# A two-layer attention and GEGLU kernel: first row tile in fp32 from raw weights, seven more transposed on TensorE, all loads in one queue, and a new order

## The chip, the core and the metric

The kernel runs on one core of a Trainium2 chip. A core has five engines with instruction streams of their own: TensorE (PE, matrix products; its weight loads are listed as PEld), VectorE (DVE), ScalarE (ACT), GpSimd (POOL) and SyncE (SP, which here only issues transfers). TensorE reads SBUF and writes PSUM; 16 DMA engines move data between HBM and SBUF. SyncE and ScalarE each have a DMA queue. The metric is the time of one execution on the device in microseconds; lower is better.

## What is computed

Two layers over x of 2048 rows and 512 columns in fp32, with the same weights in both: x is normalised, goes through attention and is added back; it is normalised again, goes through a gated feed forward and is added back.

```python
def _A_ref(x, wqkv, wo):          # D = 512, H = 32 heads of 16
    W, dil = 8, 2
    qkv = (x @ wqkv)              # split into q, k, v
    idx = pos[:, None] - off[None, :]      # off = 0, 2, ..., 14
    logits = jnp.einsum("bhsd,bhswd->bhsw", q, kg) * scale
    logits = jnp.where(mask, logits, -1e9)
    attn = _softmax(logits, axis=-1)
    o = jnp.einsum("bhsw,bhswd->bhsd", attn, vg)
    return o_as_rows @ wo
def _B_ref(x, w_gate, w_up, w_down):       # F = 1792
    return (_gelu(x @ w_gate) * (x @ w_up)) @ w_down
x = A_x
x = x + _A_ref(_layernorm(x), A_wqkv, A_wo)
x = x + _B_ref(_layernorm(x), B_w_gate, B_w_up, B_w_down)
# and both once more
```

Each position looks at itself and at seven positions before it, two apart. So even and odd rows never meet in attention, and the kernel treats them as two sequences of 1024.

## The kernel before

**Tiles.** Each layer is cut into eight chunks of two row tiles of 128 rows (`CHUNKS`, even and odd rows in turn, J = 2). A chunk goes through three functions:

- `attention_inputs(l, c, prio)`: loads the chunk's rows tile by tile into `xa` (three buffers), takes their mean and variance (`norm`: VectorE for the statistics, then a short chain for the inverse root, on VectorE for the very first chunk and on GpSimd for the others, one chain for both tiles), and calls `normed` for each tile. That writes the normalised tile `xn` on ScalarE, and `split_transpose` makes of it two f16 halves, `hl`: the rounded value (ScalarE) and the remainder (GpSimd, L777). A DMA transpose (SyncE, L781) turns both into `ax`, with the contraction on the partitions. The projection to q, k, v is done for each half of the heads, h, and each tile, j: 12 matmuls of 512 and 12 of 256 columns (L801): high times high, high times low and low times high, over four blocks of the contraction. ScalarE moves the result out of PSUM (L840, `stg`), and SyncE stores it to `qkvd` in HBM (L851).
- `attention(l, c, T)`: for each of four groups of eight heads loads windows of q, k and v from `qkvd` (L878) with their halo of earlier rows, and does logits, softmax and the weighted sum on VectorE (with the exponential on ScalarE). The result is split and turned by a DMA transpose into `ot`.
- `feed_forward(l, c, T, ot, mark)`: the output projection with `w_o`, the residual, a norm, a DMA transpose into `bx`, then seven steps of gate and up products into PSUM `pg`, gelu and product, a split into `gh`, and the down products into `pd`; the sum goes to `xs` (layer 0) or `out` (layer 1).

**Weights.** All matmuls work in f16 with split operands. Each weight is loaded raw in fp32, its largest magnitude is found (`absmax` on VectorE or `abssum` on ScalarE), a power of two is made of it (`exponents`: reductions, transposes on PE at L398, small VectorE operations), and `split` writes the scaled high half (ScalarE, L443) and the low half (VectorE, L448) in f16. wqkv comes in two halves of four blocks each (`prep_q(0)` and `prep_q(1)`), and its raw blocks lie in the buffer of `w_d`. The loads of wqkv are issued by SyncE; those of the gate, up, output and down weights by ScalarE (`on="ACT"` in `load`, L482): 16 of 448 KB, 4 and 14 of 256 KB.

**The halo of the first rows.** The rows ahead of the sequence in `qkvd` are filled with zeros by eight DMAs that ScalarE issues (L636).

**The order.** Nothing is emitted at once. Every step is a node in a graph with an engine, an estimated occupancy, what it reads and writes, the buffers it takes, and a priority. `plan` places the nodes one after another: each time the one that could start earliest by its model; among those that could start within a short time of that, the one of lowest priority. The instructions are then emitted in that order, and every engine works through its own in order. The priorities come from the table `AT`; `ahead` (8.5 tiles) says for how many tiles of layer 0 the inputs of attention have a place of their own ahead of the feed forward. `start` and `step` set the nominal times T of the chunks. `plan` models the DMA engines as a rate of 370 bytes per ns, shared by two queues, with a limit on how much is queued ahead in each.

Of the kernel before, what the change touches and what calls it, by code (L numbers as in the profile page):

```python
# [17 lines left out]
P = 128  # L18
# [72 lines left out]
DMA_FIXED = 1.8  # L91
QUEUE = {"SP": 3.0, "ACT": 1.0}
DEPTH = 3.6
WAIT, SOON = 0.3, 20.0
DMA_RATE = 0.37e3


class Graph:
# [4 lines left out]
    def add(self, where, occ, fn, r=(), w=(), prio=0.0, get=(), order=(), done=None, kb=None, table=None, urgent=False, after=0.0):  # L103
# [3 lines left out]
        n.land, n.size, n.urgent, n.after = done, kb, urgent, after  # L107
# [40 lines left out]
    def plan(self):  # L148
# [15 lines left out]
        dma, port_free, table = {"SP": 0.0, "ACT": 0.0}, 0.0, None  # L164
        placed, todo = [], len(self.nodes)
        while todo:
            best = None
            for e, ns in cand.items():
                at = []
                for n in ns:  # L170
                    t = max(free[e], n.ready, port_free if n.port else 0.0)
                    if n.size is not None and not n.urgent:
                        t = max(t, dma[e] - QUEUE[e])
# [31 lines left out]
            if n.size is not None:  # L205

                other = "ACT" if e == "SP" else "SP"
                free[e] = max(free[e], dma[e] - DEPTH)
                begin = max(t + occ, dma[e])
                both = min(max(0.0, dma[other] - begin), 2 * n.size / DMA_RATE)  # L210
                dma[e] = begin + n.size / DMA_RATE + both / 2
                dma[other] += both / 2
                n.done = dma[e] + DMA_FIXED
            else:
                n.done = t + (occ if n.land is None else occ - n.occ + n.land) + LAG[e]
# [40 lines left out]
def t_mm(n):  # L256
    return 0.0025 + n / 2400


T_SMALL = 0.17  # L260
T_ISSUE = 0.45
T_XPOSE = 1.3
LATE = 1e6
# [3 lines left out]
def dilated_attention_geglu(ctx: ExitStack, tc: tile.TileContext, x, wqkv, wo, wg, wu, wd, out):  # L267
# [99 lines left out]
    P_st = pool("stg", 3, [P, 3, HH, P])  # L367
# [11 lines left out]
    P_pr = Pool("prod", [prod], fifo=False)  # L379
    pd_flat = P_pd.tiles[0].rearrange("p j c -> p (j c)")  # L380
# [98 lines left out]
    def load(dst, src, kb, w, prio, r=(), on="SP"):  # L479
        eng = nc.sync if on == "SP" else nc.scalar  # L480
        return g.add(
            on, T_ISSUE, lambda: eng.dma_start(dst, src), r=r, w=w, kb=kb, prio=prio,  # L482
            after=AT["bulk"] if on == "ACT" else 0.0,
        )
# [20 lines left out]
    def prep_q(h, prio, early):  # L505
# [18 lines left out]

        g.add("DVE", 3 * T_SMALL, rest, r=[(f"q{h}", "e")], w=[("s_log", h)], prio=prio + 50)
# [4 lines left out]
    def load_f(h, prio):  # L530
        for k in range(KT):
            for key, w, src in (("g", w_g, wg), ("u", w_u, wu)):
                src = src.rearrange("(k p) (h c) -> h k p c", p=P, h=2)
                i = h * KT + k
                load(w.raw(i), src[h, k], 448, [(f"r{key}", i)], prio + 0.1 * k, on="ACT")

    def prep_f(h, prio, how):
# [17 lines left out]
        for k in range(KT):  # L555
            for n, (key, w) in enumerate((("g", w_g), ("u", w_u))):
                i = h * KT + k
                pre = [(key, i - 1)] if i else []
# [21 lines left out]
    def prep_o(prio, how, early):  # L580
        for k in range(KT):
            load(w_o.raw(k), wo[k * P : (k + 1) * P], 256, [(P_o_lease, k)], early, on="ACT")
# [13 lines left out]
    def load_d(prio):  # L596
        for i in range(NF):
# [3 lines left out]
                r=[("q", b) for b in range(2 * KT)], on="ACT",  # L601
# [22 lines left out]
    zeros = P_k.tiles[0].rearrange("p r c -> p (r c)")[0:16, 0 : HALO * P]  # L624
    z_lease = Lease(P_k)
    for l in range(2):
        dst = qkvd[l].rearrange("a h t r c -> (a h) t r c")[:, 2:6, 0:HALO]
        if l == 0:
            g.add(
                "POOL", 1.6, lambda: nc.gpsimd.memset(zeros, 0.0), w=[(z_lease, 0)],  # L630
                get=[z_lease], prio=-2000,
            )
        for a in range(4):
            g.add(
                "ACT", 0.35,
                lambda dst=dst, a=a: nc.scalar.dma_start(  # L636
# [535 lines left out]
```

## Time and profile before

| | |
|---|---|
| runs | 1274.81, 1277.32, 1278.92 us, median 1277.32 |
| span of the profiled execution | 1280.5 us |
| PE busy | 1226.0 us, 96% |
| VectorE busy | 994.7 us, 78% |
| ScalarE busy | 488.4 us, 38% |
| GpSimd busy | 402.0 us, 31% |
| mean granted TensorE clock | 0.988 |
| moved by DMA | 176.09 MB |

A row of a timeline has the start in us, the duration, the engine, the line of the kernel, the operation, what it writes and reads, shapes, a count where several are merged, and in brackets how long the engine was idle before and what ended that. The names are the program's own: `ax<-hl` is the DMA transpose of an attention input, `qkvd<-stg` a store of projections, `xa` a loaded row tile; raw wqkv blocks appear as `w_d`, in whose buffer they lie. A group row ends with busy us and the mean ns of one, and the idle time before. The chain of waits has the start, the duration, and what the end of the kernel was waiting for in that time. Matmuls are pipelined and their ends are modelled: in a dense stretch the distance of starts, not the duration, is what one costs.

### The profile page before, as it was taken

Reading aid. Unit: us, or ns where it says so; the run is one execution under the profiler, and the core shown is the slowest. Engines: PE = TensorE matmul, PEld = TensorE weight load, DVE = VectorE, ACT = ScalarE, POOL = GpSimd, SP = SyncE. Lnnn points to the kernel's source line nnn. Section 1 sums busy time; section 2 is a strip of 40 time slices with the busy share of each in tenths; the row PEclk is TensorE's granted clock in tenths of the full one; section 3 lists DMA queues with packets and bytes.
Section 4 is the critical chain, followed back from the end, with each engine's and each line's share of the span. In section 5 each row is a group of like instructions: output and inputs, shape, how many; then the busy total and the mean of one; then the engine's idle time right before and its main releaser. Section 6 shows DMA issues by size and latency. Waiting matters only on the chain.

```text
span 1280.5 us, 21381 instructions
## 1 busy us (share of the span) xinstructions
PE 1226.0 (96%) x8650; PEld 848.9 (66%) x8650; DVE 994.7 (78%) x1435; ACT 488.4 (38%) x746; POOL 402.0 (31%) x388
## 2 busy tenths in 40 slices
PE   3689799999999999999999999999999999999998
PEld 1345367586767676765776676767766676676775
DVE  5568889998898989998988958888888788685111
ACT  4366265343434444333433243333334242332211
POOL 2233227443243423431433142322313222042211
PEclk9899899999999999999999999999999999999999
DMA  9999952554545372529534393334354262621000
GB/s 236 266 280 329 227 158 81 142 160 117 172 101 164 97 211 82 152 84 247 140 99 126 110 241 93 105 101 130 105 151 120 85 186 44 202 62 42 17 17 17
DMA packets 201794, 176.09 MB, mean 138 GB/s; under 512 B 108224, under 2 KB 168640, under 8 KB 201696
## 3 DMA queue, kind: packets, MB, share of 16 engines
q1 hardware_dynamic: 196736, 162.57, 45.7%
q10 hardware_dynamic: 4960, 12.18, 3.5%
q8 instruction: 67, 1.10, 0.4%
q14 instruction: 31, 0.25, 0.1%
HBM read 115.87 MB, written 33.67 MB: 117 GB/s over the span
## 4 chain that ended last, share of the span: by engine, by line
PE 90%; DMA 8%; DVE 1%; SPq 1%; ACT 0%; issue 0%; POOL 0%; DVEq 0%; ACTq 0%
PE pg L801 67%; PE pd L1089 23%; DMA ax<-hl 3%; DMA qkvd<-stg 2%; DMA xa<-in_A_x_dram 1%; DMA v<-qkvd 1%; DMA w_d<-in_A_wqkv_dram 0%; DMA bx<-hl 0%; ACT stg L840 0%; DVE x L1102 0%; SPq L878 0%; SPq L482 0%; SPq L781 0%; DVE x L1008 0%; DVE nw L697 0%
## 5 line engine op out<-in xcount | busy, mean ns | idle before, releaser
L801 PE MATMUL pg<-bx,w_g 128*128 128x256 f16 x2688 | 330.0, 273 | 0.4 <-DMA bx<-hl 0.4
L801 PE MATMUL pg<-bx,w_u 128*128 128x256 f16 x2688 | 330.1, 273 | 0.0
L1089 PE MATMUL pd<-w_d,gh 128*128 128x512 f16 x1344 | 306.7, 379 | 0.0
L801 PEld LDWEIGHTS <-w_g 128*128 128x128 f16 x2688 | 262.8, 98 | 49.1 <-issue 0.6
L801 PE MATMUL pg<-w_q,ax 128*128 128x512 f16 (+1 forms) x1536 | 267.6, 336 | 28.1 <-DMA ax<-hl 23.4
L1078 POOL TENSOR_TENSOR gh<-g,gh 128x512 f16<-128x512 f32 x112 | 166.1, 1483 | 409.2 <-ACT gh L1073 406.2
L801 PEld LDWEIGHTS <-w_u 128*128 128x128 f16 x2688 | 262.8, 98 | 30.6
L801 PEld LDWEIGHTS <-ax 128*128 128x128 f16 x1536 | 153.0, 100 | 142.7 <-DMA ax<-hl 27.9
L1089 PEld LDWEIGHTS <-gh 128*128 128x128 f16 x1344 | 131.4, 98 | 139.9
L1064 DVE SCALAR_TENSOR_TENSOR g<-pg,small,g 128x512 f32<-128x512 f32 (+1 forms) x128 | 85.8, 681 | 141.1 <-ACT g L1056 138.9
L1056 ACT ACTIVATE g<-pg,small 128x512 f32<-128x512 f32 (+1 forms) x128 | 79.4, 633 | 270.7 <-PE pg L801 260.3
L955 DVE TENSOR_TENSOR prod<-v,lg 128x1024 f32<-128x1024 f32 x128 | 168.7, 1349 | 1.2
L777 POOL TENSOR_TENSOR hl<-xn,hl 128x512 f16<-128x512 f32 x64 | 86.5, 1358 | 237.8 <-ACT hl L773 213.6
L896 DVE TENSOR_TENSOR prod<-k,q 128x2048 f32<-128x2048 f32 x64 | 148.6, 2322 | 7.0 <-DMA k<-qkvd 6.3
L966 DVE TENSOR_TENSOR prod<-prod 128x1024 f32<-128x1024 f32 (+1 forms) x128 | 150.6, 1176 | 1.6
L903 DVE TENSOR_REDUCE lg<-prod 128x128 f32<-128x2048 f32 x64 | 145.9, 2279 | 0.9
L777 POOL TENSOR_TENSOR hl<-o,hl 128x256 f16<-128x256 f32 x64 | 79.0, 1235 | 176.3 <-ACT hl L773 166.7
L840 ACT ACTIVATE stg<-pg 128x768 f32<-128x768 f32 x64 | 51.2, 807 | 128.1 <-PE pg L801 125.1
L1073 ACT CAST gh<-g 128x512 f16<-128x512 f32 x112 | 68.9, 616 | 78.8 <-DVE g L1064 75.5
L801 PE MATMUL pg<-w_o,ot 128*128 128x512 f16 x384 | 85.5, 379 | 0.0
L1056 ACT ACT_TABLE_LOAD x41 | 52.6, 1283 | 34.4 <-PE pg L801 34.0
L801 PEld LDWEIGHTS <-ot 128*128 128x128 f16 x384 | 37.6, 98 | 42.1
(78 smaller groups left out, 678.8 us busy)
## 6 DMA issues: line engine op xcount, KB each, us to landing
k<-qkvd SPq DMA_DIRECT2D x64, 576.0 KB, 5.3
v<-qkvd SPq DMA_DIRECT2D x64, 576.0 KB, 3.5
qkvd<-stg SPq DMA_DIRECT2D x64, 384.0 KB, 4.8
q<-qkvd SPq DMA_DIRECT2D x64, 128.0 KB, 2.3
xa<-in_A_x_dram SPq DMA_DIRECT2D x16, 256.0 KB, 4.5
x<-in_A_x_dram SPq DMA_DIRECT2D x8, 512.0 KB
xs<-x SPq DMA_DIRECT2D x8, 512.0 KB, 3.5
xa<-xs SPq DMA_DIRECT2D x16, 256.0 KB, 5.9
```

The lines of the kernel that those rows point to most:

```text
L777: "POOL", t_pool(n), lambda: nc.gpsimd.tensor_sub(lo(), src(), hi()),
L801: nc.tensor.matmul(pt, a, b, start=i == 0, stop=i == n - 1)
L840: lambda pg=pg, stg=stg: nc.scalar.activation(stg.tile().rearrange("p t g c -> p (t g c)"), pg.tile().rearrange("p b c -> p (b c)")[:, 0:768],
L896: nc.vector.tensor_mul(pr, win, q.tile()[:, 0:J].unsqueeze(2).to_broadcast([P, J, W, P]))
L903: lambda lgv=lgv: nc.vector.tensor_reduce(lgv(), pr.rearrange("p j w (h d) -> p j w h d", d=DH), axis=AX.X, op=ALU.add),
L955: lambda j=j, v=v, lg=lg: nc.vector.tensor_mul(prod[:, j].rearrange("p w (h d) -> p w h d", d=DH), v.tile()[:, j : j + W].rearrange("p w ( ...
L966: lambda a=a, b=b: nc.vector.tensor_add(pr[:, :, 0:a], pr[:, :, 0:a], pr[:, :, a:b]),
L1056: lambda sel=sel, h=h, pg=pg, gt=gt: nc.scalar.activation(gt.tile()[:, sel, 0:N], pg.tile()[:, sel, 0:N], AF.Gelu_apprx_tanh, scale=cst["s ...
L1064: lambda sel=sel, h=h, pg=pg, gt=gt: nc.vector.scalar_tensor_tensor(gt.tile()[:, sel, 0:N], pg.tile()[:, sel, JM * P : JM * P + N], cst["c ...
L1073: lambda gt=gt, gh=gh: nc.scalar.copy(gh.tile()[:, 0, :, 0:N], gt.tile()[:, :, 0:N]),
L1078: lambda gt=gt, gh=gh: nc.gpsimd.tensor_sub(gh.tile()[:, 1, :, 0:N], gt.tile()[:, :, 0:N], gh.tile()[:, 0, :, 0:N]),
L1089: nc.tensor.matmul(pd.tile()[:, j], gh.tile()[:, a, i, cs], wd_of(f, b), start=f == 0 and n == 0, stop=f == NF - 1 and n == 2,)
```

## The change

- **First row tile.** `NRAW` = 1: tile 0 of layer 0 is projected with fp32 matmuls from the raw weights. A new `turned` makes `xn` as before and transposes its four blocks on PE into a PSUM buffer of `pg`; `turned_whole` moves the result to `xf` in SBUF, a piece of `w_g`'s buffer that isn't written until the two projections are done (`("x0", h)`). The projection has 8 matmuls for each half of the heads in place of 24, and the scale that the split would have applied to the weights is applied when ScalarE empties PSUM (`s_raw`).
- **Tiles 1 to 7** of layer 0 (`NPE` = 8): the transposes are done on PE as well; ScalarE writes the f16 high part from PSUM, and VectorE the remainder. The GpSimd subtraction and the DMA transpose of these tiles go.
- **The first chunk** has a norm for each of its two tiles, on VectorE for the first and on GpSimd for the second.
- **Loads**: all are issued by SyncE. The zero fill is one DMA per layer.
- **The model of `plan`** has one DMA queue; each transfer has a time for its shape (x 1.55 us for two tiles, a store of projections 1.25, k and v 1.65, q 0.4, a transpose of four blocks 0.96, weights by 330 bytes per ns). `AT` has new numbers throughout; `ahead` is 17.1 tiles. `stg` buffers are no longer taken strictly in turn.

```diff
-    lq0=-1.2, lq1=-1.3, lf0=5.0, lo=42.0, lf1=44.3, ld=60.0, pq0=-787.8, pq1=9.2, pf0=26.2, po=53.4, pf1=62.0,
-    pd=130.5, x0=-1000.0, first=-1.4, tile=12.1, ahead=8.5, lead=190.5, norm=300.0, proj=10.1, half=18.4,
-    row=12.4, att=90.0, hg1=6.5, hg2=12.0, kv=13.7, xl=28.1, gu=5.4, bulk=8.0, start=51.1, step=39.1,
+    lq0=-167.4, lq1=-34.0, lf0=-158.4, lo=122.2, lf1=232.9, ld=421.6, pq0=-172.6, pq1=-218.4, pf0=-37.8,
+    po=-41.1, pf1=67.7, pd=70.0, x0=-1490.1, first=-77.3, tile=6.1, ahead=17.1, lead=339.3, norm=23.4,
+    proj=-32.1, half=129.8, row=-113.0, att=76.2, hg1=9.7, hg2=7.9, kv=-12.0, xl=406.6, gu=5.9, bulk=167.5,
+    start=28.2, step=41.3,
...
-    def load(dst, src, kb, w, prio, r=(), on="SP"):
-        eng = nc.sync if on == "SP" else nc.scalar
+    def load(dst, src, kb, w, prio, r=()):
         return g.add(
-            on, T_ISSUE, lambda: eng.dma_start(dst, src), r=r, w=w, kb=kb, prio=prio,
-            after=AT["bulk"] if on == "ACT" else 0.0,
+            "SP", T_ISSUE, lambda: nc.sync.dma_start(dst, src), r=r, w=w, us=kb / RATE, prio=prio,
         )
...
+    def turned(x_of, norm_l, scale_bias, j, prio, get=()):
+        xn = scaled(x_of, norm_l, scale_bias, j, prio)
+        lease = Lease(P_pg)
+        view = lambda: lease.tile()[:, 0].rearrange("p (k c) -> p k c", k=KT)
+        def turn():
+            for k in range(KT):
+                nc.tensor.transpose(view()[:, k], xn.tile()[:, k * P : (k + 1) * P], ident)
+        g.add("PE", T_TURN, turn, r=[(xn, 0)], w=[(lease, 0)], get=[lease, *get], prio=prio)
+        return lease, view
...
+    def turned_split(x_of, norm_l, scale_bias, j, dst, w, get, prio):
+        pt, view = turned(x_of, norm_l, scale_bias, j, prio, get)
+        g.add(
+            "ACT", t_act(D), lambda: nc.scalar.copy(dst()[:, 0], view()),
+            r=[(pt, 0)], w=w, prio=prio,
+        )
+        g.add(
+            "DVE", t_dvp(D), lambda: nc.vector.tensor_sub(dst()[:, 1], view(), dst()[:, 0]),
+            r=[(pt, 0)], w=w, prio=prio,
+        )
...
+                def project_whole(h=h, pg=pg, xf=xf):
+                    pt = pg.tile().rearrange("p b c -> p (b c)")
+                    for kt in range(KT):
+                        for lo, hi in span:
+                            nc.tensor.matmul(
+                                pt[:, lo:hi], xf.tile()[:, kt * P : (kt + 1) * P],
+                                w_q.raw(h * KT + kt)[:, lo:hi], start=kt == 0, stop=kt == KT - 1,
+                            )
...
+        cst["s_raw", h], mk_raw = power(e, -1, 268 + LQ)
...
+        if l + c == 0:
+            norms = [norm([xt[j]], prio - AT["norm"] + j, "POOL" if j else "DVE") for j in range(J)]
+            norms = [(nl, lambda j, f=f: f(0)) for nl, f in norms]
+        else:
+            norms = [norm(xt, prio - AT["norm"], "POOL")] * J
```

More of the change, by code (lines that the diff above doesn't have):

```diff
@@ L101, in __init__, with add @@
         self.writer, self.readers = {}, {}
-    def add(self, where, occ, fn, r=(), w=(), prio=0.0, get=(), order=(), done=None, kb=None, table=None, urgent=False, after=0.0):
+    def add(self, where, occ, fn, r=(), w=(), prio=0.0, get=(), order=(), done=None, us=None, table=None, urgent=False, after=0.0):
         n = Node()
@@ L163, in plan @@
         free = dict.fromkeys(LAG, 0.0)
-        dma, port_free, table = {"SP": 0.0, "ACT": 0.0}, 0.0, None
+        dma, port_free, table = 0.0, 0.0, None
         placed, todo = [], len(self.nodes)
@@ L205, in plan @@
             if n.size is not None:
[L207 to L213, printed above, removed]
+                free[e] = max(free[e], dma - DEPTH)
+                dma = max(t + DMA_ISSUE, dma) + n.size
+                n.done = max(dma + DMA_FIXED, t + occ + DMA_FIXED)
             else:
@@ L262 @@
 T_XPOSE = 1.3
+T_TURN = 0.8
+NRAW, NPE = 1, 8
 LATE = 1e6
@@ L534, in load_f @@
                 i = h * KT + k
-                load(w.raw(i), src[h, k], 448, [(f"r{key}", i)], prio + 0.1 * k, on="ACT")
+                load(w.raw(i), src[h, k], 448, [(f"r{key}", i)], prio + 0.1 * k)
     def prep_f(h, prio, how):
@@ L581, in prep_o @@
         for k in range(KT):
-            load(w_o.raw(k), wo[k * P : (k + 1) * P], 256, [(P_o_lease, k)], early, on="ACT")
+            load(w_o.raw(k), wo[k * P : (k + 1) * P], 256, [(P_o_lease, k)], early)
         for k in range(KT):
@@ L600, in load_d @@
                 w_d.raw(i), wd[i * P : (i + 1) * P], 256, [("rd", i)], prio + 0.1 * i,
-                r=[("q", b) for b in range(2 * KT)], on="ACT",
+                r=[*(("q", b) for b in range(2 * KT)), ("x0", 0), ("x0", 1)],
             )
@@ L819, in attention_inputs @@
                 pg, stg = Lease(P_pg), Lease(P_st)
+                whole = n0 + j < NRAW
+                span = ((0, 512), (512, 768))
                 def project(h=h, j=j, pg=pg):
```

123 lines of the change are left out of this document (78 added, 45 removed).

## The prediction

> **What bounds the kernel now.** I read the windows of the trace first, cut where TensorE (PE) stops being full, then PE's timeline, then the chain of waits. Columns of the windows: stretch, us, busy time of PE, its weight loads (PEld), VectorE, ScalarE and GpSimd with their instructions, granted clock of PE, mean share of the 16 DMA engines, GB/s.
>
> ```profile
> 0.00:42.00 42.00, 12.20 (x51) 5.85 (x52) 23.49 (x59) 18.68 (x27) 11.28 (x30) 0.97 1.06 224
> 42.00:162.00 120.00, 101.20 (x561) 56.61 (x560) 91.26 (x161) 59.84 (x107) 34.31 (x50) 0.91 1.02 282
> 162.00:1275.00 1113.00, 1112.63 (x8040) 786.43 (x8040) 878.50 (x1215) 409.85 (x613) 356.39 (x308) 1.00 0.42 119
> ```
>
> From 162 to 1275 us PE has 1112.6 of 1113 us of work: nothing but less PE work can shorten that part. Before 162 the DMA engines are full and PE is not. How much PE time is lost there has to be counted in PE's pace, since busy time holds the modelled ends of matmuls. The groups by form give the counts, the end of the chain the pace:
>
> ```profile
> L801 PE MATMUL pg<-bx,w_u 128*128 128x256 f16 x2688 | 330.1, 273 | 0.0
> L801 PE MATMUL pg<-bx,w_g 128*128 128x256 f16 x2688 | 330.0, 273 | 0.4 <-DMA bx<-hl 0.4
> L1089 PE MATMUL pd<-w_d,gh 128*128 128x512 f16 x1344 | 306.7, 379 | 0.0
> L801 PE MATMUL pg<-w_q,ax 128*128 128x512 f16 x768 | 188.1, 398 | 28.1 <-DMA ax<-hl 23.4 <-ACT stg L840 2.5 <-DVE lg L930 2.3
> L801 PE MATMUL pg<-w_q,ax 128*128 128x256 f16 x768 | 95.5, 275 | 0.0
> L801 PE MATMUL pg<-w_o,ot 128*128 128x512 f16 x384 | 85.5, 379 | 0.0
> L398 PE MATMUL pg<-ident,small 128*128 128x128 f32 x10 | 2.5, 312 | 20.5 <-DVE small L391 20.5
> ```
>
> ```profile
> 1261.98 5.24 PE pg L801 x48
> 1267.22 7.78 PE pd L1089 x36
> ```
>
> 48 matmuls of 256 columns in 5.24 us are 0.1092 each, 36 of 512 columns in 7.78 us are 0.2161 each. So 6144 x 0.1092 + 2496 x 0.2161, and about 1 us for ten small fp32 ones, are **1211.4 us of work**. The last matmul ends at 1275.0; 5.5 us of eviction and store follow, to the span of 1280.5. The rest, 1275.0 - 1211.4 = **63.6 us, is lost**. PE's timeline (start, us, what, idle before and its releaser) says where:
>
> ```profile
> 16.07 0.45 PE L398 MATMUL pg<-ident,small 128*128 128x128 f32 x1 [16.07 <-DVE small L391]
> 22.95 11.02 PE L801 MATMUL pg<-w_q,ax 128*128 128x512 f16 x48 [2.43 <-DMA ax<-hl]
> 41.75 13.93 PE L801 MATMUL pg<-w_q,ax 128*128 128x512 f16 x72 [7.77 <-DMA ax<-hl]
> 55.51 0.38 PE L398 MATMUL pg<-ident,small 128*128 128x128 f32 x2
> ...
> 72.42 17.46 PE L801 MATMUL pg<-w_q,ax 128*128 128x512 f16 x96 [4.21 <-DMA ax<-hl]
> ...
> 99.73 7.97 PE L801 MATMUL pg<-w_q,ax 128*128 128x512 f16 x48 [0.78 <-DMA ax<-hl]
> 108.20 19.68 PE L801 MATMUL pg<-w_q,ax 128*128 128x512 f16 x120 [0.49 <-DMA ax<-hl]
> 135.60 14.78 PE L801 MATMUL pg<-w_q,ax 128*128 128x512 f16 x72 [7.72 <-DMA ax<-hl]
> 150.21 5.34 PE L801 MATMUL pg<-w_o,ot 128*128 128x512 f16 x24
> ```
>
> Half a row tile of QKV is 24 matmuls, 12 x (0.2161 + 0.1092) = 3.90 us. Before 41.75 PE did two halves, 7.8 us, and 0.2 of transposes: 33.7 lost. From there to 162 the window and the counts give 22 halves (85.8), the first output projection (24 x 0.2161 = 5.2) and 0.9 of transposes: 28.3 lost. That is 62 of the 63.6. The large gaps end with ax<-hl, the DMA transpose of a normalised row tile. The chain of waits says that it is slow as well as late, and the issue table of the whole run says what it takes in the middle:
>
> ```profile
> 14.46 15.39 DMA ax<-hl
> ```
>
> ```profile
> ax<-hl SPq DMA_TRANSPOSE x32, 3.4
> ```
>
> 15.4 us amid the weight loads, 3.4 in the middle case. These transposes, and what they wait for, are what bounds the start.
>
> **The change part by part.** The rows for it are of the timeline:
>
> ```profile
> 1.65 7.62 SPq L482 DMA_DIRECT2D w_d<-in_A_wqkv_dram  x8
> 4.13 0.69 DVE L697 BATCH_NORM_STATS2 nw<-xa 128x6 f32<-128x512 f32 x1 [4.13 <-DMA xa<-in_A_x_dram]
> 5.28 0.69 DVE L697 BATCH_NORM_STATS2 nw<-xa 128x6 f32<-128x512 f32 x1 [0.46 <-DMA xa<-in_A_x_dram]
> ...
> 8.39 0.16 DVE L746 SCALAR_TENSOR_TENSOR nw<-nw 128x2 f32<-128x2 f32 x1
> ...
> 10.11 0.80 ACT L790 ACTIVATE xn<-xa,nw 128x512 f32<-128x512 f32 x1
> ...
> 20.62 3.81 DVE L448 SCALAR_TENSOR_TENSOR w_q<-w_d,small,w_q 128x768 f16<-128x768 f32 x4 [0.63 <-ACT w_q L443]
> ...
> 27.62 0.15 PEld L801 LDWEIGHTS <-ax 128*128 128x128 f16 x1 [0.28 <-issue]
> ...
> 36.09 5.96 ACTq L482 DMA_DIRECT2D prod<-in_A_wo_dram  x2
> ```
>
> ```profile
> L1008 DVE SCALAR_TENSOR_TENSOR x<-pg,small,x 128x512 f32<-128x512 f32 x32 | 22.5, 745 | 16.4 <-PE pg L801 13.4 <-DMA x<-xs 2.7
> ```
>
> *First row tile in fp32.* It needs neither a DMA transpose nor split weights. With a norm of its own it no longer waits for the second tile's statistics, 5.28 - 4.13 = 1.15 us: bias at 8.55 - 1.15 = 7.4. Then 0.80 on ScalarE, four transposes, and 0.75 for VectorE to move 512 columns out of PSUM (the row of L1008): first matmul near **10.3** in place of 22.95. The transposes are like the fp32 pair at 55.51: two take 0.38, one alone 0.27 (0.312 in the mean), so 0.11 a piece, 0.44 a tile. The trace shows no fp32 projection. Half a tile streams 4 x 768 = 3072 columns, 24 times 128: at 0.11 that is 2.6 us, at the cold single 0.45 of 16.07 it is 10.8. I take twice the warm pace, 5.3, nearer to the warm row because only the first few meet a PE that has idled. Two halves are 10.6 for 7.8, **+2.8 us of work** (ends -2.6 and +13.8). The Trainium skill (FP8 and Floating Point Precision, TensorE Precision Notes) counts four passes for true fp32; the pair at 55.51 runs at the pace of two, so the two would differ by 5.2 us in the sum, which no run here decides yet.
>
> *Seven more tiles turned on PE.* Eight turns at 0.44 add **+3.5 us of work** (by the mean of 0.312 apiece 10.0, the upper end; none is the lower). Eight DMA transposes, GpSimd's subtractions and as many f16 copies go; a ScalarE copy out of PSUM takes the copy's place, and VectorE gets a subtraction that reads PSUM, 8 x 0.75 = 6 us. VectorE is busy 114.8 of the first 162 us, so its slack hides them; without it they cost those 6. A turn that waits for xn holds the matmuls queued behind it on PE, and takes one of the three PSUM buffers of the projections; I leave that among the stalls.
>
> *Loads in SyncE's queue.* All 34 that ScalarE issued leave it; there two took 5.96 us at 36.09 because the queue was full, and the work behind them stood. On SyncE they now stand ahead of stores, xa loads and transposes. The order is laid out for it, so the forecast counts no loss; the loss is a rival.
>
> *Order.* QKV of all 16 tiles of layer 0 is pulled forward (limit 17.1 tiles, before 8.5). The gap of 7.72 before 135.60 is tile 10, the first beyond the old limit. This must carry PE until the first feed forward: 10.3 + 16 x 7.8 + 6.3 = 141, with stalls some 155. The old order had chunk 0's attention projected by 150.21, so even one no earlier hardly leaves PE dry. After that VectorE's 878 us of 1113 leave it a fifth free.
>
> *Zero fill, a freer stg pool, two more constants.* Fewer issues on ScalarE and four small VectorE operations of 0.15: nothing, since the zeros are next read by chunk 0's attention, long after.
>
> *The sum.* Work: 1211.4 + 2.8 + 3.5 = 1217.7. Lost early: 10.3 to the first matmul; 2.5 at the slow pace (the weight loads of the first tile stood 0.43 apart, 0.15 and 0.28, from 22.95 to 28.05, twelve at half pace, though the granted clock reads 0.97); 5 between the end of the raw half, near 16, and split weights for the second tile, which came at 24.4 (20.62 + 3.81) and should come by some 21: 17.8 for 33.7. Lost later: 28.3, less the 13.2 of the four gaps at 72, 99, 108 and 135, less some 5 of half pace behind them: 10. Tail: 5.5. **1217.7 + 17.8 + 10 + 5.5 = 1251.0** for the profiled execution; that of before stood 3.2 above the median of the runs (1280.5, 1277.3), so **1248**. Loss may rise from 27.8 to 57 before the gain is gone.
>
> **The rivals.**
>
> *Only the beginning gains.* The later 28.3 would be DMA bandwidth, which the change leaves. For it: a DMA share of 1.02 up to 162. Against: eight transposes go, and the gaps end with them. 1217.7 + 17.8 + 28.3 + 5.5 = 1269 profiled, 1266.
>
> *One queue blocks: slower.* Eight wqkv loads took SyncE 7.62 us to issue, 0.95 each. With three such ahead of each store and each xa load of a tile, 3 x 2.9 = 8.6 us a tile, over PE's 7.8: from there on PE waits for SyncE. For it: SyncE waits in order, and ax<-hl was the chain. Against: the xa buffers hold three tiles. Four us uncovered for each of eight tiles on top of 27.8: lost 60, 1283 profiled, 1280; more if the weights come later too. The Trainium skill (DMA: Bandwidth & Descriptors, Queues, rings and completion order) says that a DMA engine serves its queues in turn, packet by packet. By that, a store on SyncE used to pass between ScalarE's bulk packets and now stands behind them; the 15.4 us of a transpose amid loads fits the taking of turns, and says that it was no favour.
>
> *Fully fed.* The later stalls vanish too: lost 13 to 17, about 1238 profiled, 1235.
>
> **How the numbers follow.** Forecast (lost 16 to 42, 1236 to 1262 as a median) 0.64; only the beginning 0.18; one queue blocks 0.10; fully fed 0.08. The range 1235 to 1269 holds the forecast with the bounds of the fp32 tile, most of the second case and half of the last: 0.8. A measurement of this kernel tells about 0.3% from no change, so faster is below 1273.5: 0.64 + 0.08 + 0.13 = 0.85; same 0.05; slower 0.10.
>
> **What would show it.** First QKV matmul by 12; the fp32 ones of 512 columns 0.88 us apart; no gap of PE ended by ax<-hl before the ninth tile; first output projection by 155 and PE full from there. It is wrong if gaps of PE end with qkvd<-stg or xa, if the first feed forward comes after 165, or if PE has gaps later because attention is late.

## The result, and the profile after

| | before | after |
|---|---|---|
| runs, median (lowest to highest) | 1277.32 us (1274.81 to 1278.92) | **1254.04 us** (1253.26 to 1255.47) |
| span of the profiled execution | 1280.5 us | 1252.3 us |
| ratio of the times, 95% interval | | 0.9826 (0.9807 to 0.9845) |

The change makes the kernel 1.7% faster, 23.3 us. Forecast were 1248.0 us and a range from 1235 to 1269.

First the windows of the changed kernel, cut at the same 42 and 162 us, with the columns of before: stretch, us, busy time of PE, weight loads, VectorE, ScalarE, GpSimd, clock, DMA share, GB/s.

```profile
0.00:42.00 42.00, 26.85 (x105) 15.81 (x106) 31.56 (x80) 21.37 (x35) 8.06 (x34) 0.96 0.96 333
42.00:162.00 120.00, 117.99 (x735) 71.67 (x733) 115.72 (x182) 75.93 (x131) 47.49 (x62) 1.00 0.96 275
162.00:1246.00 1084.00, 1079.02 (x7829) 765.48 (x7827) 846.79 (x1185) 398.78 (x587) 355.04 (x292) 1.00 0.41 117
```

Between 42 and 162 us PE was busy 101.2 us before and is busy 118.0 now, while the DMA engines are about as full (1.02 and 0.96). So bandwidth was not what starved PE there. VectorE is where the new load sits: 115.7 of 120 us, from 91.3.

PE's timeline (start, us, what, idle before and its releaser):

```profile
10.41 1.97 PE L808 MATMUL pg<-ident,xn 128*128 128x128 f32 x8 [10.41 <-ACT xn L788]
...
14.56 7.33 PE L890 MATMUL pg<-w_d,w_g 128*128 128x512 f32 x16
21.73 4.06 PE L837 MATMUL pg<-w_q,ax 128*128 128x512 f16 x24
28.21 0.72 PE L808 MATMUL pg<-ident,xn 128*128 128x128 f32 x4 [2.42 <-ACT xn L788]
28.73 7.00 PE L890 MATMUL pg<-w_d,w_g 128*128 128x512 f32 x16
...
76.57 27.46 PE L837 MATMUL pg<-w_q,ax 128*128 128x512 f16 x168 [0.71 <-DVE ax L830]
...
124.59 7.97 PE L837 MATMUL pg<-w_q,ax 128*128 128x512 f16 x48 [0.52 <-DMA ax<-hl]
132.40 5.34 PE L837 MATMUL pg<-w_o,ot 128*128 128x512 f16 x24
```

Tiles 0 and 1 are turned together at 10.41. The fp32 halves of tile 0 are the two rows of L890; the split matmuls (L837) of tile 1 come between them. From 28.73 to the first feed forward, which begins at 157.30, no gap of PE is longer than 0.71 us, where before there were gaps of 7.77, 4.21 and 7.72. The first output projection begins at 132.40, in place of 150.21.

What PE waited for in the first 320 us (who waits for whom: us in total, times, longest), the largest entries before and then after:

```profile
PE pg L801 <- DMA ax<-hl: 23.4, 6, 7.8
PE pg L398 <- DVE small L391: 20.5, 3, 16.1
```

```profile
PE pg L808 <- ACT xn L788: 12.8, 2, 10.4
PE pd L1160 <- POOL gh L1149: 1.6, 1, 1.6
...
PE pg L837 <- DVE ax L830: 0.7, 1, 0.7
PE pg L837 <- DMA ax<-hl: 0.5, 1, 0.5
```

The wait for the DMA transposes of attention inputs fell from 23.4 us to 0.5. The wait for their replacement, VectorE's remainder at L830, is 0.7.

**The accounts.** By the pace of the prediction (0.1092 us for 256 columns, 0.2161 for 512, the fp32 work as the trace has it) the matmuls of each kernel add up to its work. What is left of the time up to the last matmul is called lost; it holds idle time and slow pace together.

| us | before | predicted | after |
|---|---|---|---|
| work of PE | 1211.4 | 1217.7 | 1217.5 |
| lost up to 42 | 33.8 | 17.8 | 20.8 |
| lost from 42 to 162 | 28.1 | 10 | 3.1 |
| lost after 162 | 1.7 | 0 | 5.3 |
| behind the last matmul | 5.5 | 5.5 | 5.6 |
| span | 1280.5 | 1251.0 | 1252.3 |
| median of the runs | 1277.3 | 1248 | 1254.0 |

### The profile page after: what moved, and what is told of

Its sections match the earlier page's. It is cut to its first block, busy times and chain, and to the rows that moved or that the text cites. A ratio compares the mean times of both kernels' runs of the same rounds, so it can differ in the third digit from the quotient of the medians.

```text
span 1252.3 us, 21416 instructions
## 1 busy us (share of the span) xinstructions
PE 1224.5 (98%) x8666; PEld 853.1 (68%) x8666; DVE 995.5 (79%) x1447; ACT 496.1 (40%) x751; POOL 410.6 (33%) x388
## 4 chain that ended last, share of the span: by engine, by line
PE 88%; DVE 5%; DMA 4%; SPq 1%; ACT 1%; issue 1%; POOL 0%; DVEq 0%; ACTq 0%
PE pg L837 64%; PE pd L1160 23%; DMA ax<-hl 2%; PE pg L890 1%; DMA w_g<-in_B_w_gate_dram 1%; DVE prod L967 1%; DVE prod L1026 1%; DVE lg L974 1%; DMA ot<-hl 0%; DVE prod L1037 0%; SPq L481 0%; DMA bx<-hl 0%; DVE w_g L448 0%; DVE nw L695 0%; DVE w_u L448 0%
## 5 line engine op out<-in xcount | busy, mean ns | idle before, releaser
L837 PE MATMUL pg<-bx,w_g 128*128 128x256 f16 x2688 | 330.1, 273 | 2.1 <-DMA bx<-hl 2.1
L837 PE MATMUL pg<-bx,w_u 128*128 128x256 f16 x2688 | 330.1, 273 | 0.0
L1149 POOL TENSOR_TENSOR gh<-g,gh 128x512 f16<-128x512 f32 x112 | 172.0, 1535 | 465.3 <-ACT gh L1144 458.9
L837 PEld LDWEIGHTS <-w_g 128*128 128x128 f16 x2688 | 263.0, 98 | 49.8 <-issue 2.4
L837 PEld LDWEIGHTS <-w_u 128*128 128x128 f16 x2688 | 263.0, 98 | 30.4
L837 PE MATMUL pg<-w_q,ax 128*128 128x512 f16 x1488 | 248.6, 326 | 3.5 <-DMA ax<-hl 1.6
L837 PEld LDWEIGHTS <-ax 128*128 128x128 f16 x1488 | 145.2, 98 | 106.5 <-issue 3.1
L967 DVE TENSOR_TENSOR prod<-k,q 128x2048 f32<-128x2048 f32 x64 | 152.7, 2386 | 0.7
L1037 DVE TENSOR_TENSOR prod<-prod 128x1024 f32<-128x1024 f32 (+1 forms) x128 | 143.2, 1118 | 1.6
L775 POOL TENSOR_TENSOR hl<-xn,hl 128x512 f16<-128x512 f32 x56 | 74.6, 1341 | 130.4 <-ACT hl L771 117.8
L837 PE MATMUL pg<-w_o,ot 128*128 128x512 f16 x384 | 85.7, 379 | 0.2 <-DMA ot<-hl 0.2
L837 PEld LDWEIGHTS <-ot 128*128 128x128 f16 x384 | 37.5, 98 | 43.4 <-DMA ot<-hl 0.7
```

Of the source, the lines that this page charges most:

```text
L775: "POOL", t_pool(n), lambda: nc.gpsimd.tensor_sub(lo(), src(), hi()),
L837: nc.tensor.matmul(pt, a, b, start=i == 0, stop=i == n - 1)
L967: nc.vector.tensor_mul(pr, win, q.tile()[:, 0:J].unsqueeze(2).to_broadcast([P, J, W, P]))
L1037: lambda a=a, b=b: nc.vector.tensor_add(pr[:, :, 0:a], pr[:, :, 0:a], pr[:, :, a:b]),
L1149: lambda gt=gt, gh=gh: nc.gpsimd.tensor_sub(gh.tile()[:, 1, :, 0:N], gt.tile()[:, :, 0:N], gh.tile()[:, 0, :, 0:N]),
```

## The experiments

Eleven kernels were run, each beside runs of the kernel before on its own chip; those had medians of 1276.0 (chip of e1 to e4), 1276.6 (e5 to e8) and 1276.9 us (e9 to e11), close to the 1277.3 of the result. The table has the median of each and the same accounts. The accounts are of the one profiled execution, which can lie off the median: 4.3 us above it in e4, 7.3 below in e5. The changed kernel and its variants ran on different chips, so a difference of 3 us between them is near the limit of what the intervals tell apart.

| kernel | median us (lowest to highest), runs | ratio to before, interval | lost to 42 | 42 to 162 | after 162 |
|---|---|---|---|---|---|
| changed | 1254.0 (1253.3 to 1255.5), 4 | 0.9826 (0.9807 to 0.9845) | 20.8 | 3.1 | 5.3 |
| e1 | 1257.1 (1256.3 to 1258.3), 4 | 0.9853 (0.9824 to 0.9883) | 22.7 | 4.8 | 3.9 |
| e2 | 1266.6 (1262.2 to 1267.8), 5 | 0.9922 (0.9896 to 0.9949) | 23.8 | 15.2 | 5.7 |
| e3 | 1338.0 (1336.1 to 1339.0), 4 | 1.0485 (1.0453 to 1.0516) | 27.1 | 77.2 | 8.9 |
| e4 | 1282.7 (1280.6 to 1286.9), 10 | 1.0045 (1.0027 to 1.0064) | 33.3 | 10.1 | 24.7 |
| e5 | 1275.0 (1267.7 to 1283.6), 10 | 0.9998 (0.9970 to 1.0026) | 26.9 | 16.3 | 2.8 |
| e6 | 1272.9 (1270.9 to 1274.1), 6 | 0.9969 (0.9957 to 0.9981) | 25.6 | 7.8 | 17.5 |
| e7 | 1277.4 (1275.0 to 1279.7), 10 | 1.0012 (0.9992 to 1.0032) | 21.8 | 14.5 | 17.7 |
| e8 | 1268.6 (1267.9 to 1268.8), 4 | 0.9935 (0.9919 to 0.9952) | 25.2 | 14.6 | 3.7 |
| e9 | 1257.2 (1256.9 to 1258.0), 4 | 0.9849 (0.9827 to 0.9871) | 22.9 | 6.0 | 4.5 |
| e10 | 1253.6 (1252.6 to 1254.6), 4 | 0.9820 (0.9798 to 0.9842) | 20.8 | 3.7 | 4.5 |
| e11 | 1279.9 (1275.2 to 1282.2), 11 | 1.0020 (1.0002 to 1.0038) | 25.6 | 14.2 | 14.4 |

Two kinds of edit must be kept apart. e1, e2, e5, e9 and e10 keep the order of the changed kernel as it stands and put something else in its places. In the others `plan` lays the order out anew, and such a run tests the part and the new order together.

### e1: the weight loads back in ScalarE's queue, same order

```diff
-            "SP", T_ISSUE, lambda: nc.sync.dma_start(dst, src), ...
+            "SP", T_ISSUE, lambda: (nc.sync if kb == 384 else nc.scalar).dma_start(dst, src), ...
```

(384 KB blocks are those of wqkv; they stay with SyncE.)

> The 34 loads of the gate, up, output and down weights go back to ScalarE's queue, at the same places in an otherwise unchanged order. Theory A (PE no longer waits for DMA transposes; the queue is secondary): ScalarE's work stands behind full-queue issues, PE loses 3 to 8 us more before 162 us, 1257 to 1262 us. Rival Q (the single queue made the gain, because ScalarE no longer blocks and small packets no longer take turns with bulk): most of the 23 us is lost, 1268 us or more, with PE gaps that end in stg or ax. By the Trainium skill (DMA: Bandwidth & Descriptors, Issuing engines are not separate DMA queues) only issue time changes hands, and the time would stay at 1254.

Measured: 1257.1 us, 3.1 above the changed kernel, and the lowest of its runs is above the highest of the other, though the intervals of the two ratios overlap. The number is the lower end of theory A; its reason is not what the trace shows. ScalarE takes the magnitude of two of the first four wqkv blocks. Here is the second, which the exponent of this half waits for, with the idle time before it, in the changed kernel and then in e1:

```profile
11.72 0.82 ACT L497 ACTIVATE pd<-w_d 128x768 f32<-128x768 f32 x1 [0.67 <-DMA w_d<-in_A_wqkv_dram]
```

```profile
15.64 0.81 ACT L498 ACTIVATE pd<-w_d 128x768 f32<-128x768 f32 x1 [4.87 <-DMA w_d<-in_A_wqkv_dram]
```

The wqkv blocks come later while gate and up blocks are sent beside them: the longest load into that buffer before 30 us takes 10.8 us from issue to landing, against 8.0. PE's first projection begins at 17.42 in place of 14.56, and the output projection at 136 in place of 132. ScalarE itself was not held up by its issues, as theory A had it: the longest of a weight load took 0.97 us. So the one queue is worth some 3 us here, as an order of arrival.

The Trainium skill (DMA: Bandwidth & Descriptors, Issuing engines are not separate DMA queues) says that transfers begun by several engines interleave on the same DMA engines, and that spreading the issue only saves issue time. The interleaving fits this run, where the longest landing is 10.8 us in place of 8.0. But more than issue time changed here: blocks that nobody needs yet arrive among those that the start waits for, and the time is 3 us longer.

### e2: tiles 1 to 7 by DMA transposes, same order

```diff
+            if by_dma is not None:          # tiles 1 to 7
+                nc.scalar.copy(hl[:, 0:D], xn.tile())
+                nc.gpsimd.tensor_sub(hl[:, D : 2 * D], xn.tile(), hl[:, 0:D])
+                nc.sync.dma_start_transpose(by_dma().rearrange("p t k c -> p (t k) c"), hl)
+                return
             for k in range(KT):
                 nc.tensor.transpose(...)
```

ScalarE's copy and VectorE's subtraction from PSUM go for these tiles.

> Tiles 1 to 7 get their DMA transposes back (ScalarE's f16 copy, GpSimd's subtraction and the transpose issued where the turn on PE stood); order, queue and the fp32 tile as in the changed kernel. PE work falls by about 3 us. Theory A: PE waits for ax<-hl again, each turn about 4 us later, seven of them partly uncovered: 1262 to 1272 us. Rival Q (transposes were slow only because bulk loads in the other queue took turns with them): in one queue each takes about 3 us and the three tiles of lead hide it: 1250 to 1257.

Measured: 1266.6 us, 12.5 above the changed kernel, though PE has 3.1 us less to do; between 42 and 162 us it loses 12.1 more. What PE waited for in the first 320 us, two rows of SyncE's issues (start, us, what), two of ScalarE's timeline, and three of the chain of waits up to 75 us:

```profile
PE pg L817 <- ACT xn L788: 11.2, 1, 11.2
PE pg L846 <- DMA ax<-hl: 11.2, 5, 5.6
```

```profile
62.58 1.24 SPq L814 DMA_TRANSPOSE ax<-hl  x1
65.74 1.24 SPq L814 DMA_TRANSPOSE ax<-hl  x1
```

```profile
62.58 0.81 ACT L788 ACTIVATE xn<-xa,nw 128x512 f32<-128x512 f32 x1 [3.30 <-POOL hl L813]
65.75 0.81 ACT L788 ACTIVATE xn<-xa,nw 128x512 f32<-128x512 f32 x1 [2.35 <-POOL hl L813]
```

```profile
60.59 5.14 POOL hl L813 x2
...
68.11 0.43 ACT stg L919
68.53 5.64 DMA xa<-in_A_x_dram
```

The view of the tile `ax` up to 80 us ends with the time from issue to landing of those transposes whose landing it knows, three of five:

```profile
DMA to landing us min/median/max: 3.5/3.8/4.9
```

The transposes themselves are not slow any more: 3.8 us in the middle case, where the same view of the kernel before has a single such time, 11.3. They are late. Each waits for GpSimd's subtraction (two of them, 60.59 to 65.73, are in the chain). Two engines stand for it. SyncE waits for it at the transposes, 16.0 us in seven waits up to 165 us, with loads and stores behind. ScalarE waits for it before the next `xn`, 3.30 and 2.35 us; its `stg` comes behind that, and the chain puts the load of a later row tile, `xa` at 68.53, down to ScalarE and not to SyncE's order. So the 12.5 us are the price of a step that waits in two streams with other work, more than that of a slow transfer; how much each stream costs is not separated. And the order was made for turns on PE, so 12.5 is what the turns are worth in this order, not against the best order for DMA transposes.

### e5: e1 and e2 together

Both edits in one kernel: DMA transposes beside a second queue, as the kernel before had it, in the new order.

> As e2 (tiles 1 to 7 by DMA transpose, order otherwise that of the changed kernel) and, as in e1, with the 34 loads in ScalarE's queue. Theory A: the two losses add, 1254 + 12.5 + 3, 1267 to 1272, and the early transposes again take 7 us or more from issue to landing, against the 3.5 to 4.9 that e2 shows in one queue. Rival Q (the turns on PE are worth anything only beside one queue, since bulk of a second queue is what slows a transpose): the sum is exceeded, 1275 or more. If the queue makes no difference to a transpose: 1264 to 1268.

Measured: 1275.0 us in the median, but its ten runs lie between 1267.7 and 1283.6, and the profiled one is the lowest of them (span 1265.9, 13.6 above the changed kernel). Its transposes up to 80 us, from issue to landing:

```profile
DMA to landing us min/median/max: 4.3/5.1/7.2
```

They are slower than the 3.5/3.8/4.9 of e2. The median is 20.9 above the changed kernel, where the two edits one by one add 15.6. It lies above the range of theory A and just at the bound of rival Q, and the spread covers both, so this run does not decide whether the two losses simply add. It allows no more than that the two together give back most of the gain of 23.3.

### e3: the new tiles in the old planner's order

```diff
-    lq0=-167.4, lq1=-34.0, ... ahead=17.1, ...
+    lq0=-1.2, lq1=-1.3, ... ahead=8.5, ...
-DMA_ISSUE, DMA_FIXED = 0.35, 1.45
-QUEUE = 3.0
+QUEUE = {"SP": 3.0, "ACT": 1.0}
-    def load(dst, src, kb, w, prio, r=()):
+    def load(dst, src, kb, w, prio, r=(), on="SP"):
```

`AT`, the model of two queues, the loads on ScalarE and `stg` in turn are those of before; the fp32 tile and the seven turned tiles stay.

> The fp32 tile and the seven turned ones, with the old planner, its old priorities and the loads in ScalarE's queue. Theory A: the first QKV matmul comes near 14 us in place of 23 and the gaps ended by ax<-hl before tile 8 go, the one at tile 10 stays: 1260 to 1268. Rival O (the new order made the gain): no faster than before, 1274 to 1284, since PE has 6 us more to do.

Measured: 1338.0 us, slower than before by 4.9% and beyond every number expected. PE's largest gap, and the end of the chain of waits that leads to it:

```profile
169.55 7.33 PE L843 MATMUL pg<-w_o,ot 128*128 128x512 f16 x24 [44.75 <-DVE ax L836]
```

```profile
164.57 1.06 DVE w_g L452
...
166.70 2.20 DVE lg L980
168.90 0.61 DVE ax L836
169.55 2.72 PE pg L843 x6
```

L836 is the remainder of a turned tile, 0.61 us of work. In VectorE's list it stands behind splits of the weights and steps of attention, and PE stood 44.75 us for it. The next largest gap of PE, 19.78 us before 105.67, also ends with VectorE, at a reduction for the exponent of a weight (L410). The turn took the work off GpSimd and SyncE and put it in VectorE's, which has the least room after PE's. With the old priorities, and the order that `plan` made of them, it does not pay; in the changed kernel's order it does.

### e4: the old tiles in the new order

```diff
-NRAW, NPE = 1, 8
+NRAW, NPE = 0, 0
```

> The new planner, priorities and single queue, with all sixteen tiles of layer 0 split and turned by DMA as before. Theory A: first QKV matmul at 20 us or later and gaps ended by ax<-hl, less the one at tile 10: 1264 to 1274. Rival O: within 5 us of the changed kernel, 1250 to 1259.

Measured: 1282.7 us, 0.45% slower than before; both expectations missed. Up to 162 us it loses 43.4, less than the 61.9 of before, and then 24.7 more. What PE waited for up to 320 us:

```profile
PE pg L837 <- DMA ax<-hl: 17.7, 6, 6.8
...
PE pg L837 <- DMA bx<-hl: 8.1, 2, 5.7
PE pg L837 <- ACT w_g L443: 3.6, 1, 3.6
PE pg L837 <- DVE w_g L448: 3.0, 1, 3.0
```

The first feed forwards now come before their inputs and the splits of their gate weights.

### e6, e7 and e11: less of the change, or a truer estimate, with the order laid out anew

e6 turns only tile 0 (`NRAW, NPE = 1, 1`), e7 has no fp32 tile (`NRAW, NPE = 0, 8`), e11 has the whole change, and `plan` is told what a turn takes by the trace:

```diff
-T_TURN = 0.8
+T_TURN = 0.44
```

> NPE = 1: the fp32 tile stays, tiles 1 to 7 by DMA transposes, and the planner lays its order out for that (new priorities, one queue). Theory A (turning on PE takes away waits that no order hides): 1260 to 1270, as e2. Rival O (e2 lost because its order wasn't made for transposes): 1251 to 1257.

> NRAW = 0: all eight first tiles are turned on PE and projected from split weights, order laid out anew by the same planner and priorities. PE has 2.5 us less to do, and the first QKV matmul comes at 21 to 22 (the split of the first half of wqkv ends at 21.05) in place of 14.6. Theory A (the fp32 tile earns what it fills): the 7 us of the first fp32 half are lost again, less its 2.5 us: 1257 to 1263. Rival: the second half of wqkv, which lands near 28, is what the start waits for, and the fp32 tile only moves the wait: 1251 to 1256.

> The planner's estimate of a turn on PE is 0.44 us (measured) in place of 0.8; nothing else is changed, but the order is laid out anew. If the order follows the model and a truer model gives a better order: 1250 to 1256. If an order laid out anew is a draw among orders whose times differ by many us, with the priorities fitted to one of them (as e6 to e8 suggest): 1260 or more.

Measured: 1272.9, 1277.4 and 1279.9 us. For e6 and e7 both expectations are missed, and e11 is where its second one had it. All three lose 14 to 18 us after 162 us, where the changed kernel loses 5.3. A row of PE's waits for each, of e6, e7 and e11 in turn:

```profile
PE pg L837 <- ACT w_g L443: 8.1, 2, 5.5
```

```profile
PE pg L837 <- ACT w_g L443: 4.1, 1, 4.1
```

```profile
PE pg L837 <- DVE w_g L448: 4.7, 1, 4.7
```

A part of it, 4 to 8 us, is again gate weights that are split too late. In e11 the instructions are the same as in the changed kernel, a number of the model is nearer to the truth, and it costs 25.8 us, all the gain. So e6 and e7 say little of the part that they leave out, and the same holds for e3 and e4. What e11 shows is that the gain is that of the new tiles together with one order: the numbers of `AT` go with that order, and an edit through `plan` tries another one.

### e8: the second half of wqkv loaded sooner, with the order laid out anew

```diff
-    lq0=-167.4, lq1=-34.0, ...
+    lq0=-167.4, lq1=-163.0, ...
```

> One priority changed: the second half of wqkv is loaded before the first halves of gate and up, not after them (lq1 -34 to -163). If its landing near 28 us is what ends PE's gap at 25.8: that gap (2.4 us) and the half pace behind it (3.4 us of the second fp32 half cost 1.7) go, 1249 to 1252. If the loads of gate and up, then about 4.7 us later, delay the first feed forward or VectorE's reductions instead: 1254 to 1262.

Measured: 1268.6 us; both expectations missed. PE's timeline has two new gaps:

```profile
39.12 1.12 PE L808 MATMUL pg<-ident,xn 128*128 128x128 f32 x4 [6.95 <-ACT xn L788]
...
87.78 32.45 PE L837 MATMUL pg<-w_q,ax 128*128 128x512 f16 x183 [8.23 <-DVE ax L830]
```

Both fp32 halves now stand one behind the other, from 14.91, but tile 2 is turned only at 39.12, in place of 28.21, and later PE waits for VectorE's remainder. This order loses 3.7 us after 162, less than the changed kernel, so the 14 to 25 of the other new orders don't come with every one; the loss before 162 grows to 39.8.

### e9: the first half of tile 0 from split weights, the rest in the same order

```diff
+                    if h == 0:     # 24 f16 matmuls, as for the other tiles
+                        passes(pt[:, lo:hi], [(xh[:, 0, kt], wq(kt, w_q.hi)) ...])
+                        return
```

VectorE also writes tile 0 in two f16 parts, and this half's projection stands right ahead of that of tile 1.

> Order not laid out anew: in the changed kernel's order, the first half of the heads of tile 0 is projected from the split weights (24 matmuls), right ahead of that of tile 1, where it stood alone as fp32; VectorE makes the two f16 halves beside the fp32 copy (1.4 us). The second half stays fp32. Theory A (7.2 us of PE time at 14.6 are filled by it): PE idles until 21.5, does both halves at first at half pace, and everything behind moves by some 5 us: 1258 to 1261. Rival (the start waits for the second half of wqkv and the tile loaded third, both near 28, and PE's gap of 2.4 us at 25.8 takes up what the fp32 half saved): 1254 to 1256.

Measured: 1257.2 us, 3.1 above the changed kernel and between the two ranges expected. PE's first projection:

```profile
18.24 0.59 PE L845 MATMUL pg<-w_q,gh 128*128 128x512 f16 x1 [4.14 <-ACT w_q L443]
```

It begins 3.68 us later, when the first split block is there. So the raw weights of the first half buy some 3 us, in which VectorE's two extra steps are counted: not the 8 by which PE starts earlier than it did in the kernel before, since the split is ready at 21 in the changed kernel anyway.

### e10: the first tile out of PSUM sooner, the rest in the same order

In the changed kernel VectorE has an item ahead of the copy of the turned tile 0 (L818), the maximum over a gate block whose load is still on its way. Its timeline there:

```profile
12.75 1.08 DVE L487 TENSOR_REDUCE small<-w_g 128x1 f32<-128x896 f32 x1 [2.08 <-DMA w_g<-in_B_w_gate_dram]
...
13.82 0.68 DVE L818 COPY w_g<-pg 128x512 f32<-128x512 f32 x1
```

e10 moves such maxima behind the copy:

```diff
+    last = max(g.moved, g.subs[0], key=order.index)      # the copy, tile 1's remainder
+    early = [n for n in g.maxes if order.index(n) < order.index(last)]
+    for n in early:
+        order.remove(n)
+    at = order.index(last) + 1
+    order[at:at] = early
```

> Order not laid out anew but for one step: VectorE's first maximum over a gate block, which waits for its load until 12.75, comes behind the copy out of PSUM that the first projection waits for. The first fp32 matmul comes at 13.2 to 13.6 in place of 14.6. If the time of the first matmul counts: 1253. If the waits behind it (split of wqkv at 21.05, the gap at 25.8) count: no change, 1253.5 to 1255.

Measured: 1253.6 us, the same as the changed kernel, as the second expectation had it. The first projection begins at 13.31 in place of 14.56. PE's timeline of e10, and the end of the norm of tile 2 in its chain of waits:

```profile
13.31 8.25 PE L895 MATMUL pg<-w_d,w_g 128*128 128x512 f32 x16
21.40 4.06 PE L842 MATMUL pg<-w_q,ax 128*128 128x512 f16 x24
28.22 0.66 PE L811 MATMUL pg<-ident,xn 128*128 128x128 f32 x4 [2.76 <-ACT xn L791]
```

```profile
27.08 0.25 POOL nw L764
```

Most of the 1.25 us is gone within the first half itself, which takes 8.09 us (13.31 to 21.40) in place of 7.17: PE's slow pace ends near the same time in both, 19.0 and 18.4 us, by the start of the clock's record (see the last section). The remaining 0.33 goes at the next wait: tile 2 is turned at 28.22, as it is without the edit (28.21). Its norm ends on GpSimd at 27.33, and at 26.93 in the changed kernel. There it was ScalarE's list that let tile 2 through, at 27.36; its rows:

```profile
25.82 0.81 ACT L910 ACTIVATE stg<-pg 128x768 f32<-128x768 f32 x1 [3.00 <-PE pg L837]
...
27.36 1.51 ACT L788 ACTIVATE xn<-xa,nw 128x512 f32<-128x512 f32 x2
```

Two things end within 0.4 us of each other there, so taking time off one of them gains 0.4 at most.

## Why the prediction held, and where its sizes were off

**The account of PE held.** All kernels here differ by up to 84 us in time and by 6 us at most in work, so the change acts on what PE loses, as the prediction said, against 6 us of added work. That work and loss add up to the time is no test, since the loss is what is left over. And the loss need not lie at the start: e4, e6, e7 and e11 lose 14 to 25 us after 162.

**Work: +6.3 predicted, +6.1 counted.** Two rows of weight loads from the second half, where PE runs at full pace, show one block of the contraction:

```profile
32.12 0.19 PEld L890 LDWEIGHTS pg<-w_d,w_g 128*128 128x128 f32 x1 [0.49 <-issue]
...
33.41 0.19 PEld L890 LDWEIGHTS pg<-w_d,w_g 128*128 128x128 f32 x1 [0.24 <-issue]
```

From 32.12 to 33.41 are 1.29 us for 768 columns, 0.86 for 512 (0.88 was foreseen); four blocks make 5.16 a half, where 5.3 was put. Each fp32 matmul stands in the trace as two instructions. The Trainium skill (FP8 and Floating Point Precision, TensorE Precision Notes) counts four passes for true fp32: 4 x 768 columns at the pace of the f16 ones, 0.2161 + 0.1092, are 1.30, so the trace agrees, and the fp32 transposes at 0.11 were no measure for it.

**Lost up to 42: 17.8 predicted, 20.8 measured.** The sum came out near, its terms did not. The first matmul was put at 10.3 and came at 14.56, so the bound of 12 set for it was missed. The steps listed for it add up to 9.4 only (7.4 + 0.80 + 0.44 + 0.75); 0.9 of the 10.3 has no term. And they were counted as if VectorE and ScalarE did nothing else; both work in order on other things too. The norm chain ended at 9.14 where 7.4 was counted, and the copy stood behind the maximum that e10 moves. Slow pace was put at 2.5 and was 3.7: the two fp32 halves took 7.17 and 6.83 us (14.56 to 21.73, 28.73 to 35.56) for 5.16 each. Against that, the wait of 5 us for split weights did not come at all: they were ready at 21.05 (17.24 + 3.81), before the raw half ended. In its place PE waited 2.42 us for the third row tile. That tile was not late in loading: VectorE took its statistics only at 21.95, behind the split that ends at 21.05, and the norm and ScalarE's list follow. e10 shows that the 1.25 us by which the maximum delays the first matmul cost nothing: what ends near 28 decides.

**ScalarE's 5.96 us.** The prediction read the row at 36.09 of the kernel before as two loads held by a full queue. In that trace each of the two issues took 0.33 us. The second began at 41.72. It waits for the semaphore of the DMA transpose issued at 30.37, which landed at 41.70, after 11.3 us. So ScalarE stood for a transpose there. No run shows that a full queue holds up ScalarE.

**Lost from 42 to 162: 10 predicted, 3.1 measured.** The mechanism was right, the gaps ended with the DMA transposes and left with them (e2 brings 12.1 us of them back). The prediction kept too much of the old stalls. VectorE's slack hid the subtractions as it said, in this order: PE waited 0.7 us for them in the first 320 us, but 49.3 in e3 and 9.8 in e8.

**Lost after 162: 0 predicted, 5.3 measured.** "PE full from there" holds to 0.5% only. The groups name one of the new gaps:

```profile
L837 PE MATMUL pg<-bx,w_g 128*128 128x256 f16 x2688 | 330.1, 273 | 2.1 <-DMA bx<-hl 2.1
```

A further 1.6 us is the wait for GpSimd's `gh` in the table of waits. The first output projection begins 17.8 us earlier than before, so PE asks for later inputs sooner; that they are not always ready for this reason is argued, not tried. Gaps later, from late attention, were named as a sign of error; here it is late feed-forward inputs, at some 5 us.

**From the profile to the median: -3.2 predicted, +1.7 measured.** This is the term that was mis-sized, 4.9 of the 6.0 us by which 1248 is too low. In the list of runs each time is 1.9 to 2.0 us above the span of its own execution (1254.21 and 1252.3, 1253.26 and 1251.3). So the execution of before with a span of 1280.5 took about 1282.4 us: it was 5.1 above the median, and above the highest of the listed runs, 1278.92. That excess belongs to that execution, and the prediction carried it over to a kernel that doesn't have it. The profiled times themselves, 1251.0 and 1252.3, differ by 1.3, and that is luck in part: the three losses were off by +3.0, -6.9 and +5.3, which cancel.

**The rivals.** That only the beginning gains is refuted by the second window. That one queue blocks is refuted by the time, far from its 1280, and by e1: two queues are 3 us slower. Its mechanism, SyncE waiting in order while loads stand behind, shows when a transpose waits in the one queue (e2, beside ScalarE's waits). In the changed kernel the early transposes are gone. Fully fed came near between 42 and 162, not before.

**What the parts are worth.** Undone one by one in the new order: turning tiles 1 to 7 on PE costs 12.5 us, one queue 3.1, fp32 for the first half 3.1. These are prices in this order and need not add up to the 23.3: together, the first two cost 20.9 in the median (e5). Neither the tiles nor the planner's new numbers gained anything alone: with the old ones the new tiles are 84 us slower than the changed kernel (e3, with the two queues), and with the old tiles the new ones are slower than before (e4). Each of these two is a single order. So the gain is shown for the tiles and this order together, and how it divides between them is open. Not tried alone were the limit of 17.1 tiles, which the prediction held to end the gap before tile 10, the freer `stg` pool, the zero fill and the second norm. Why one new order puts the splits of gate weights late and another (e8) doesn't stays open.

## What to carry to other kernels

Add up the work of the bounding engine by its dense pace and ask what ends each gap; a step that waits for several engines and a queue may be cheaper on the bounding engine itself when that engine is idle there anyway (the turns of seven tiles are 3.1 us of work here and gain 12.5 net in their order). In a kernel whose order is laid out by a planner, test a part by replacing it in its place, since a new layout of the same instructions moved the time by 14 to 26 us (e8, e11). The price so found is that of the part in this order. Convert a profiled span by the offset that each run shows between its span and its time, and look at where the profiled execution lies among the runs before using their difference.

## What the runs showed of the hardware that was not expected

A DMA transpose in the first 80 us took 3.5 to 4.9 us from issue to landing with all loads in one queue (e2), 4.3 to 7.2 with two queues in the same order (e5), and in the kernel before 11.3 by the view of `ax` and 15.4 by the chain of waits for another.

PE's slow pace at the start shows in the granted clock only in part. Windows of the changed kernel, with the columns of before:

```profile
14.56:18.43 3.87, 3.87 (x6) 2.14 (x7) 3.19 (x14) 2.16 (x3) 0.00 (x0) 1.00 1.03 421
28.67:32.08 3.41, 3.41 (x7) 1.73 (x6) 2.81 (x5) 2.82 (x8) 0.00 (x0) 0.50 1.10 379
```

The second fp32 half lost 1.67 us (6.83 for 5.16), and 3.41 us at a clock of 0.50 are 1.7. The first lost 2.01 us with a clock of 1.00 in the view; half pace over the 3.87 us would be 1.9. But the trace's record of the clock begins at 18.43 only, and the views count the time ahead of it as 1.00. At that time the pace changes: the weight loads at 15.57 and 16.42 are 0.85 us apart, those at 19.58 and 20.00 are 0.42. So the 0.96 of the first window, and the 0.97 of the kernel before, whose record begins at 28.88, leave out the slow pace of the first matmuls.

The times of kernels spread differently: the changed kernel, e1, e9 and e10 by 1.1 to 2.2 us (four runs each), the kernel before on one chip by 10.4 (21 runs, 1268.3 to 1278.8) and e5 by 15.9 (ten runs). More runs alone widen a spread. The kernel before and e5 have DMA transposes beside a second queue at the start; that this is the cause was not tried, and e11, which has neither, spreads by 6.9 (11 runs).
